# Packed attention, mish layer and top-1 experts on one core: float32 gate logits on four column tiles, a planner that charges two engines for overlap, and a last half that ends by output quarter

## The chip, the cores and the metric

One core of a Trainium2 chip. TensorE (PE; PEld is its weight load) multiplies, VectorE (DVE), ScalarE (ACT) and GpSimd (POOL) work element by element, SyncE (SP) issues the DMAs. The metric is device time in microseconds (us), as the median of several runs. One further execution was profiled; all rows below are of it.

## The reference

```python
def _attn_ref(q, k, v, p):            # 8 batches, 8 heads, 576 tokens, head size 64, 32 packed queries
    p_packed = sm_attn(p, k, v)       # softmax attention
    return sm_attn(q, p_packed, p_packed)
...
def _moe_ref(x, w_in, w_out):         # 4608 tokens, 512 -> 2048 -> 512
    h = x @ w_in
    sp = np.where(h > 20.0, h, np.log1p(np.exp(np.minimum(h, 20.0))))
    return (h * np.tanh(sp)) @ w_out
...
def _moe2_ref(x, w_gate, w1, w2):     # 8 experts, 512 -> 1024 -> 512
    logits = x @ w_gate
    expert_idx = np.argmax(logits, axis=1)
    probs = softmax(logits); gate_w = probs[np.arange(N), expert_idx]
    for e in range(E):
        mask = expert_idx == e
        out[mask] = gate_w[mask, None] * (np.maximum(x[mask] @ w1[e], 0.0) @ w2[e])
```

All is float32. The inputs q, k and p are eight times the drawn ones.

## The kernel before

Tokens are worked in 16 halves of 288 (a half of a batch each), features lie on partitions. A float32 product is made from fp32r numbers: an operand is split into a high part (a rounded copy; names ending in h) and a low part (the original minus the high part; names ending in l), and a product takes three matmuls (high by high, high by low, low by high). So every operand costs a copy (`copy_ways`, L234 on ACT, L235 on DVE, L237 on POOL) and a subtraction (`tensor_ways`, L246, on DVE or POOL).

- The start (to about 130 us) loads the first layer's weights, which come as 64-bit words, splits them (`sgn` L402, `wi` and `a` L407/L410, `woh`, `wol`) and folds the packed values into them (`w_ps` L447, `wp` L450).
- Stage B (to about 783 us) runs the first layer for all halves: `h` (L562), mish on ACT and DVE (`z` L607, then `g` split into two parts), and the output product `x2p` (L575). Its result `x2f` goes to DRAM. Around half 6 the gates of halves 0 and 1 are worked.
- Stage C runs the second layer. For each batch one expert, the one that most of its tokens choose, is loaded (`eraw`) in eight pieces and split into `exh` and `exl`. A step is one eighth of the hidden features for one half: `h_p` (12 matmuls, L835), `g` high on ACT (L842), `g` low on DVE (`moe2_lo`, L847), then `y` (12 matmuls in four output quarters d, L855). After eight steps `os` (L861) scales the four quarters by the gate weight, and a DMA (issued at L255) writes them. The tokens of other experts are worked by a loop at the program's end, behind a branch (L1007).
- A gate: `gate_mm` (L684) multiplies x2 by the gate weights, `gate_copy` (L690) moves the logits to SBUF, `gate_turn` (L696) turns them so that tokens lie on partitions, and small DVE operations (from L702) find the maximum and the softmax weight.

The order on every engine comes from a planner (`Plan`): each step has engines that may do it, with a cost in ns for each, a due time, and buffers of rings that it takes and frees. The planner simulates the engines, and the program is written out in the order that results. A changed cost therefore moves work of every engine.

Of the kernel before, what the change touches and what calls it, by code (L numbers as in the profile page):

```python
# [45 lines left out]
class Plan:  # L46
# [26 lines left out]
    def run(self):  # L73
# [24 lines left out]
        for _ in range(len(self.steps)):  # L98
# [60 lines left out]
def packed_attention_moe_kernel(ctx, tc, pT, kT, v_main, v_tail, qT, w_in, w_out, wg, w1, w2, out):  # L159
# [48 lines left out]
    tot_i = const.tile([1, 1], I32, name="tot_i")  # L208
    wg_f = const.tile([128, 4, 8], F32, name="wg_f")
    wg16 = const.tile([128, 4, 66], F32R, name="wg16")  # L210

# [468 lines left out]
    def gate_mm(i):  # L680
        l_p, n = tile_of("o", [66, TK], name="l_p"), 0
        for d in range(4):
            for x in range(2):
                T.matmul(out=l_p, lhsT=wg16[:, d], rhs=x2s[i][x][:, d], start=(n == 0), stop=(n == 7))  # L684
                n += 1
        gst[i] = l_p

    def gate_copy(i):
        l_s = tile_of("ls", [16, TK])
        S.activation(out=l_s, in_=gst[i][0:16], func=AF.Copy)  # L690
        gst[i] = l_s

    def gate_turn(i):
        t_p = tile_of("o", [96, 3, 16], name="lt_p")
        for t in range(3):
            T.transpose(t_p[:, t, :], gst[i][:, 96 * t:96 * t + 96], ident[0:16, 0:16])  # L696
        gst[i] = t_p

    def gate_max(i):
        sg = rings["sg"]  # L700
        lg = sg.tile([96, 3, 8], F32, tag="lg", name="lg")
        V.tensor_reduce(out=lg, in_=gst[i].rearrange("p t (a e) -> p t e a", a=2), axis=AX.X, op=ALU.add)  # L702
# [65 lines left out]

    def gate(i, x2, free_x2, due, exp_after=(), exp_before=None):
# [4 lines left out]
        tu = step("PE", 93, lambda: gate_turn(i), after=[cp], takes=[("o", ("t", i))], frees=[("ls", i)], due=due)  # L774
        mx = step("DVE", 600, lambda: gate_max(i), after=[tu], frees=[("o", ("t", i))], due=due)
# [35 lines left out]
    def get_expert(b, gate_of, due_of, after=()):  # L811
        fe = step("SP", 100, lambda: find_e(b), after=[found[b], gate_of(0), *after], due=due_of(0) - 8 * US)
        for k, (p, part) in enumerate(pieces):
            due = due_of(k)
            key = ("x", b, p, part)
            ld = step("SP", 0, lambda p=p, part=part: ex_load(b, ev[b], p, part), after=[fe, gate_of(k)],
                      takes=[("raw", key)], nbytes=524288, due=due - 6 * US)
            ring = ("wa", "wb")[p // 2]
            hi = plan.step(copy_ways(lambda p=p, part=part: ex_hi(b, p, part), lambda p=p, part=part: er[b, p, part], 1024),
                           after=[ld] + ex_done.get((b, p), [])[:1],  # L820
                           takes=[(ring, ("e", b, p, x)) for x in "hl"] * (part == 0), due=due)
            lo = plan.step(tensor_ways(lambda p=p, part=part: ex_t[b, p][1][:, 2 * part:2 * part + 2], lambda p=p, part=part: er[b, p, part],
                                       lambda p=p, part=part: r32(ex_t[b, p][0][:, 2 * part:2 * part + 2]), ALU.subtract, 1024),
                           after=[hi], frees=[("raw", key)], due=due)
            ex_done[b, p] = ex_done.get((b, p), []) + [hi, lo]
# [36 lines left out]

    gms, y_in, y_out = {}, {}, {}

# [4 lines left out]
    def moe2(n, due):  # L869
# [11 lines left out]
        lo = step("DVE", 369, lambda: moe2_lo(i, f), after=[hi], frees=[("h", ("y", n))], due=due)  # L881
        for d in range(4):
            y_out[n, d] = step("PE", 399, lambda d=d: moe2_out(b, i, f, d),
                               after=ex_done[b, 2 + c] + [lo, y_out.get((n - 1, d))],
                               takes=[("acc", ("y", i, d))] * (f == 0),
                               frees=[g] + [("wb", ("e", b, 2 + c, x)) for x in "hl"]
                               * (hf == 1 and o == 3), due=due + 2 * TC + TC // 3, lag=500)
        if early:
# [26 lines left out]
    for m, (which, c) in enumerate(ORDER):  # L915
# [13 lines left out]
    wg_zero = step("Pool", 600, lambda: G.memset(wg16.rearrange("p k e -> p (k e)").bitcast(F32), 0.0), due=20 * US)  # L929
    wg_load = dma(16384, lambda: wg_f, lambda: wg, due=60 * US)  # L930
    wg_done = step("DVE", 100, lambda: V.tensor_copy(out=wg16[:, :, 0:8], in_=wg_f), after=[wg_load, wg_zero], due=60 * US)
    wg_done = step("DVE", 100, lambda: V.tensor_tensor(out=wg16[:, :, 8:16], in0=wg_f, in1=r32(wg16[:, :, 0:8]),
                                                       op=ALU.subtract), after=[wg_done], due=60 * US)

    attend(0, None, at(-10))
    for i in range(NH):
# [11 lines left out]
        if i == 6:  # L948
            for m in range(2):
                key = "g", m  # L950
                ld = dma(589824, lambda m=m: x2_load(m), lambda m=m: x2_d[halves[m]], after=[after_in(n0), x2_st[m]],
                         takes=[("x2f", key)], due=at(n0 + 8 * m))
                sp = split_x2(m, key, "raw", [ld], at(n0 + 8 * m + 4))
                b_steps.extend([ld, *sp, *gate(m, key, x2_at("raw", key), at(n0 + 8 * m + 8), sins[2 * i + 1], trig_after[2 * i + 2])])

# [26 lines left out]
    for i in range(NH):  # L982
# [6 lines left out]
        if b > 0:  # L989
            gate(i, ("x2", i), [], C0 + (8 * i - 14) * TC)  # L990
            if hf == 1:
# [93 lines left out]
```

## Time and profile before

| what | value |
| --- | --- |
| median of 3 runs | 1234.04 us (1233.6 to 1234.16) |
| profiled execution, its own time | 1231.74 us |
| its span, first to last instruction | 1229.9 us |
| mean granted TensorE clock | 0.982 of full speed |
| PE busy | 1181.8 us, 96% of the span |
| DVE, ACT, POOL busy | 56%, 50%, 25% of the span |

A row of the timeline gives the start in us, the time that the row covers, engine, line, operation, output and inputs by the program's names, tile shape, and how many instructions it joins; in brackets the idle time before it and what ended it. Matmuls overlap: a 288-column matmul lasts 0.29 us, while the next one starts 0.13 us after it.

### The profile page before, as it was taken

The page shows a single profiled execution, that of the slowest core. Times are in us where ns is not written, and L with a number is a line of the kernel's source. Part 1 is how long each engine was busy: PE and PEld are TensorE (multiplying, and loading weights), DVE is VectorE, ACT ScalarE, POOL GpSimd, SP SyncE. Part 2 cuts the span into 40 slices and gives each one's busy share as a digit, 9 for nine tenths or more (in the row PEclk, how much of TensorE's full clock was granted, in tenths as well). Part 3 has the DMA queues.
Part 4 walks back from the last instruction along what each step waited for, and adds up shares of the span by engine and source line. Part 5 has one row for each costly group of instructions (what it writes and reads, how often), then busy time and mean ns, then how long its engine had stood idle before and what let it go on. Part 6 is the DMA issues. An engine that isn't in the chain of part 4 may idle for free.

```text
span 1229.9 us, 23514 instructions
## 1 busy us (share of the span) xinstructions
PE 1181.8 (96%) x9632; PEld 1094.6 (89%) x9633; DVE 688.1 (56%) x1231; ACT 611.3 (50%) x1263; POOL 307.8 (25%) x285
## 2 busy tenths in 40 slices
PE   5788999999999999999999998999999999999997
PEld 1557899899899898998998998999999999999997
DVE  5988745645555555455445546356556574746442
ACT  3638777776786786776877866211111111111110
POOL 2555211112131121121121224023324050404210
PEclk9878999999999999999999999999999999999999
DMA  8755420420521320322222031143414141523401
GB/s 305 273 202 203 185 108 1 185 108 1 223 90 52 152 108 30 156 108 76 110 108 108 1 142 54 51 137 144 162 64 186 59 185 42 204 72 134 156 31 42
DMA packets 35098, 146.23 MB, mean 119 GB/s; under 512 B 4264, under 2 KB 4392, under 8 KB 30888
## 3 DMA queue, kind: packets, MB, share of 16 engines
q1 hardware_dynamic: 34984, 144.66, 31.9%
q8 instruction: 78, 1.28, 0.4%
q14 instruction: 36, 0.29, 0.1%
HBM read 121.52 MB, written 23.12 MB: 118 GB/s over the span
## 4 chain that ended last, share of the span: by engine, by line
PE 76%; DVE 11%; DMA 4%; issue 4%; POOL 2%; SPq 1%; ACT 1%; DVEq 0%; ACTq 0%; POOLq 0%
PE x2p L575 32%; PE h L562 16%; PE y L855 11%; PE h_p L835 10%; DVE exl L246 3%; DMA eraw<-w 3%; PE w_ps L447 3%; POOL sgn L402 1%; PE o L311 1%; DVE g L847 1%; PE o L278 1%; PE o L494 1%; PE l_p L684 1%; DVE z L607 1%; POOL exh L237 1%
## 5 line engine op out<-in xcount | busy, mean ns | idle before, releaser
L575 PE MATMUL x2p<-g,woh 128*128 128x288 f32 x2048 | 424.4, 300 | 10.6 <-DVE g L246 5.6
L575 PEld LDWEIGHTS x2p<-g,woh 128*128 128x128 f32 x2048 | 331.8, 190 | 35.6 <-issue 18.8
L575 PE MATMUL x2p<-g,wol 128*128 128x288 f32 x1024 | 305.0, 298 | 2.4 <-DVE wol L246 2.4
L562 PE MATMUL h<-hl,wp 128*128 128x288 f32 x1536 | 240.6, 304 | 6.9 <-DVE wp L450 2.8
L562 PEld LDWEIGHTS h<-hl,wp 128*128 128x128 f32 x1536 | 217.7, 194 | 30.4 <-ACT hs L234 13.9
L237 POOL TENSOR_SCALAR g<-z 128x576 fp32r<-128x576 f32 x123 | 106.9, 877 | 462.4 <-DVE z L607 287.0
L842 ACT ACTIVATE g<-h_p 128x288 fp32r<-128x288 f32 x128 | 52.5, 411 | 325.6 <-PE h_p L835 304.4
L855 PE MATMUL y<-g,exh 128*128 128x288 f32 x1024 | 211.1, 298 | 3.0 <-DVE os L861 2.9
L575 PEld LDWEIGHTS x2p<-g,wol 128*128 128x128 f32 x1024 | 194.8, 190 | 2.9 <-DVE wol L246 2.9
L855 PEld LDWEIGHTS y<-g,exh 128*128 128x128 f32 x1024 | 162.6, 188 | 7.0 <-issue 4.7
L579 ACT ACTIVATE z<-h 128x288 f32<-128x288 f32 x256 | 105.5, 412 | 119.6 <-PE h L562 112.8
L607 DVE TENSOR_TENSOR z<-z,hs 128x576 f32<-128x576 f32 x128 | 96.7, 787 | 101.0 <-ACT z L604 101.0
L835 PE MATMUL h_p<-x2h,exh 128*128 128x288 f32 x512 | 152.3, 297 | 0.7 <-DVE g L847 0.7
L835 PE MATMUL h_p<-x2l,exh 128*128 128x288 f32 x512 | 151.1, 295 | 0.0
L835 PE MATMUL h_p<-x2h,exl 128*128 128x288 f32 x512 | 150.7, 294 | 0.0
L855 PE MATMUL y<-g,exl 128*128 128x288 f32 x512 | 150.4, 294 | 0.0
L847 DVE SCALAR_TENSOR_TENSOR g<-h_p,g 128x288 fp32r<-128x288 f32 x128 | 57.9, 452 | 154.7 <-ACT g L842 154.7
L237 POOL TENSOR_SCALAR exh<-eraw 128x1024 fp32r<-128x1024 f32 x63 | 101.6, 1631 | 140.3 <-DMA eraw<-w 111.4
L246 DVE TENSOR_TENSOR g<-z,g 128x576 fp32r<-128x576 f32 x128 | 106.8, 849 | 30.4 <-POOL g L237 30.2
L246 DVE TENSOR_TENSOR exl<-eraw,exh 128x1024 fp32r<-128x1024 f32 x62 | 100.7, 1653 | 29.1 <-issue 14.5
L234 ACT ACTIVATE hs<-h 128x288 f32<-128x288 f32 x256 | 104.7, 409 | 0.0
L835 PEld LDWEIGHTS h_p<-x2h,exh 128*128 128x128 f32 x512 | 96.0, 187 | 1.7 <-DVE g L847 1.3
(132 smaller groups left out, 1368.5 us busy)
## 6 DMA issues: line engine op xcount, KB each, us to landing
eraw<-w SPq DMA_DIRECT2D x64, 512.0 KB, 6.3
wi<-wi_d SPq DMA_DIRECT2D x28, 1024.0 KB, 6.3
x2f<-x_d SPq DMA_DIRECT2D x18, 576.0 KB, 4.0
raw<-kT SPq DMA_DIRECT2D x16, 576.0 KB, 8.3
q<-qT SPq DMA_DIRECT2D x16, 576.0 KB, 5.7
x_d<-x2f SPq DMA_DIRECT2D x16, 576.0 KB, 3.2
out<-os SPq DMA_DIRECT2D x16, 576.0 KB, 3.0
raw<-v_main SPq DMA_DIRECT2D x16, 512.0 KB, 8.3
```

What stands on the lines that cost most here:

```text
L234: ways = [("ACT", (51 if psum else 93) + 0.833 * n, on(lambda d, x: S.activation(out=d, in_=x, func=AF.Copy))), ("DVE", 69 + (1.03 if psum ...
L237: ways.append(("Pool", 160 + 0.835 * n, on(lambda d, x: G.tensor_scalar(out=d, in0=x, scalar1=1.0, scalar2=1.0, op0=ALU.mult, op1=ALU.mult))))
L246: engine.tensor_tensor(out=d, in0=a(), in1=b(), op=op)
L447: T.matmul(out=t[i][quarter(x)], lhsT=pk[own[i], b, x], rhs=w_i[c][own[i], x], start=True, stop=True)
L562: T.matmul(out=h, lhsT=wp_t[b, c][:, xw, kt, 128 * o:128 * o + 128], rhs=a2[i][:, xa, kt], start=(m == 0), stop=(m == 5))
L575: T.matmul(out=accs[i, d], lhsT=w_o[c][xw][:, o, 128 * d:128 * d + 128], rhs=tiles[n]["g"][:, xg, k], start=(f == 0 and m == 0), stop=(f = ...
L579: S.activation(out=part(n, "z", k), in_=tiles[n]["p", k], func=AF.Tanh, scale=0.5)
L607: g0 = step("DVE", 669, lambda n=n, z=z: V.tensor_tensor(out=z(), in0=z(), in1=tiles[n]["hs"], op=ALU.mult), after=[si, *hc[n]], frees=[(" ...
L835: T.matmul(out=h_p, lhsT=ex_t[ek, c][xw][:, k, 128 * o:128 * o + 128], rhs=x2s[xk][xx][:, k], start=(n == 0), stop=(n == 11))
L842: S.activation(out=h[:, 0], in_=hc[xk, f], func=AF.Relu)
L847: V.scalar_tensor_tensor(out=h[:, 1], in0=h_p, scalar=0.0, in1=r32(h[:, 0]), op0=ALU.max, op1=ALU.subtract)
L855: T.matmul(out=accs[xk, d], lhsT=ex_t[ek, 2 + c][xw][:, o, 128 * d:128 * d + 128], rhs=hc[xk, f][:, xh], start=(f == 0 and n == 0), stop=( ...
```

## The change

The gate's logits are no longer made from the fp32r parts of x2. Four float32 matmuls, one for each quarter d of the 512 features, multiply `x2f` itself by 32 weight columns (8 of the gate, 24 of zeros), and each writes its own 32 partitions of `l_p`. The copy to SBUF takes 128 partitions in place of 16. `gate_turn` multiplies by a small matrix `pick`, which sums the four groups of partitions while it turns. The gates of halves 0 and 1 need no split of x2. The low parts of the first expert have DVE as their only engine. In the last half the outputs of the last two steps are written by d, with a DMA for each d. The planner adds 30% of the overlap to a DVE step that overlaps POOL work and 50% to a POOL step, and some step costs and due times differ.

```diff
+    SLOWED = dict(DVE=0.3, Pool=0.5)
...
+                if e in self.SLOWED:
+
+                    other = "Pool" if e == "DVE" else "DVE"
+                    both = min(cost, max(0.0, free_at[other] - now))
+                    cost += self.SLOWED[e] * both
+                    free_at[other] += self.SLOWED[other] * both
...
-    wg_f = const.tile([128, 4, 8], F32, name="wg_f")
-    wg16 = const.tile([128, 4, 66], F32R, name="wg16")
+    wg_f = const.tile([128, 4, 32], F32, name="wg_f")
+    nc.vector.memset(wg_f, 0.0)
+    pick = const.tile([128, 8], F32, name="pick")
+    nc.vector.tensor_reduce(out=pick, in_=ident.rearrange("p (d e) -> p e d", d=4)[:, 0:8], axis=AX.X, op=ALU.add)
...
-        l_p, n = tile_of("o", [66, TK], name="l_p"), 0
+        l_p = tile_of("o", [128, TK], name="l_p")
         for d in range(4):
-            for x in range(2):
-                T.matmul(out=l_p, lhsT=wg16[:, d], rhs=x2s[i][x][:, d], start=(n == 0), stop=(n == 7))
-                n += 1
+            T.matmul(out=l_p[quarter(d)], lhsT=wg_f[:, d], rhs=x2f[i][:, d], start=True, stop=True)
...
-        t_p = tile_of("o", [96, 3, 16], name="lt_p")
+
+        t_p = tile_of("o", [96, 3, 8], name="lt_p")
         for t in range(3):
-            T.transpose(t_p[:, t, :], gst[i][:, 96 * t:96 * t + 96], ident[0:16, 0:16])
+            T.matmul(out=t_p[:, t], lhsT=gst[i][:, 96 * t:96 * t + 96], rhs=pick, start=True, stop=True)
...
-        mm = step("PE", 981, lambda: gate_mm(i), after=x2_split_done[x2] + [wg_done], takes=[("o", ("l", i))],
-                  frees=free_x2, due=due)
+        mm = step("PE", 850, lambda: gate_mm(i), after=[ld, wg_done], takes=[("o", ("l", i))], frees=[("x2f", key)], due=due,
+                  share=0.8)
...
-                                       lambda p=p, part=part: r32(ex_t[b, p][0][:, 2 * part:2 * part + 2]), ALU.subtract, 1024),
+                                       lambda p=p, part=part: r32(ex_t[b, p][0][:, 2 * part:2 * part + 2]), ALU.subtract, 1024, b > 0),
...
-        for d in range(4):
-            y_out[n, d] = step("PE", 399, lambda d=d: moe2_out(b, i, f, d),
-                               after=ex_done[b, 2 + c] + [lo, y_out.get((n - 1, d))],
+        last, ahead[n] = i == NH - 1 and f > 5, (lo, g)
+        for d, m in [(d, m) for d in range(4) for m in ((n - 1, n) if last else (n,))] * (not last or f == 7):
+            lo, g = ahead[m]
+            y_out[m, d] = step("PE", 399, lambda d=d, f=m % 8: moe2_out(b, i, f, d),
+                               after=ex_done[b, 2 + c] + [lo, y_out.get((m - 1, d))] + [ahead[n][0]] * last,
...
-        dma(589824, lambda: out[b, hf], lambda: accs[i], after=en, frees=[("os", i)], due=due)
+        if not last:
+            dma(589824, lambda: out[b, hf], lambda: accs[i], after=en, frees=[("os", i)], due=due)
+            return
+        for d in range(4):
+            dma(147456, lambda d=d: out[b, hf][:, d], lambda d=d: accs[i][:, d], after=[en[d]], frees=[("os", i)], due=due)
```

First place, PE at the first gate, in stage B. Before, the eight matmuls of `l_p` alternate between the high and the low part of x2 (the first two of them are shown):

```order
L562 MATMUL h<-hl,wp 128x288 x24
L684 MATMUL l_p<-x2h,wg_164 66x288
L684 MATMUL l_p<-x2l,wg_164 66x288
...
L575 MATMUL x2p_4161<-g,woh 128x288 x2
L575 MATMUL x2p_4161<-g,wol 128x288
L696 MATMUL lt_p<-ident,ls 96x16 x3
```

The same place in the changed kernel:

```order
L571 MATMUL h<-hl,wp 128x288 x6
L692 MATMUL l_p<-x2f,wg_f 32x288 x4
L571 MATMUL h<-hl,wp 128x288 x12
L704 MATMUL lt_p<-pick,ls 96x8 x3
L584 MATMUL x2p_4060<-g,woh 128x288 x2
```

Four matmuls of 32 weight columns stand for eight of 66, and the turn has 8 columns in place of 16 and contracts over 128 partitions in place of 16.

Second place, the end of stage B, DVE and POOL. Before, DVE first and then POOL (`exl` and `exh` are the first expert's parts, `g` and `z` belong to the last steps of the first layer):

```order
L246 TENSOR_TENSOR exl<-eraw,exh 128x1024 x3
L607 TENSOR_TENSOR z<-z,hs 128x576 x2
L235 CAST g<-z 128x576 x2
L246 TENSOR_TENSOR g<-z,g 128x576 x2
...
L237 TENSOR_SCALAR exh<-eraw 128x1024 x4
L246 TENSOR_TENSOR exl<-eraw,exh 128x1024
L237 TENSOR_SCALAR exh<-eraw 128x1024
L246 TENSOR_TENSOR exl<-eraw,exh 128x1024
```

The changed kernel, DVE and then POOL at the same place:

```order
L255 TENSOR_TENSOR exl<-eraw,exh 128x1024 x3
L616 TENSOR_TENSOR z<-z,hs 128x576 x2
L244 CAST g<-z 128x576
L255 TENSOR_TENSOR g<-z,g 128x576 x2
...
L246 TENSOR_SCALAR exh<-eraw 128x1024 x4
L246 TENSOR_SCALAR g<-z 128x576
L246 TENSOR_SCALAR exh<-eraw 128x1024
L246 TENSOR_SCALAR g<-z 128x576
```

POOL's two `exl` are gone, and one of DVE's two copies to `g` has gone to POOL. On PE, the first step of the second layer (12 matmuls of `h_p`) stood behind the last `x2p`; it now stands ahead of the last 32 groups of `x2p`:

```order
L584 MATMUL x2p_8861<-g,woh 128x288 x2
L584 MATMUL x2p_8861<-g,wol 128x288
L843 MATMUL h_p<-x2h,exh 128x288
L843 MATMUL h_p<-x2l,exh 128x288
L843 MATMUL h_p<-x2h,exl 128x288
...
L584 MATMUL x2p_8829<-g,woh 128x288 x2
L584 MATMUL x2p_8829<-g,wol 128x288
```

Third place, DVE in stage C, over the four steps ahead of an expert's first `os`. Before:

```order
L847 SCALAR_TENSOR_TENSOR g_10315<-h_p,g_10315 128x288
L246 TENSOR_TENSOR exl<-eraw,exh 128x1024 x2
L847 SCALAR_TENSOR_TENSOR g_10356<-h_p,g_10356 128x288
L246 TENSOR_TENSOR exl<-eraw,exh 128x1024 x2
L847 SCALAR_TENSOR_TENSOR g_10396<-h_p,g_10396 128x288
L246 TENSOR_TENSOR exl<-eraw,exh 128x1024 x2
L847 SCALAR_TENSOR_TENSOR g_10431<-h_p,g_10431 128x288
L246 TENSOR_TENSOR exl<-eraw,exh 128x1024 x2
L861 TENSOR_TENSOR os<-y_10172,gm 128x288
```

The changed kernel at the same place:

```order
L855 SCALAR_TENSOR_TENSOR g_10278<-h_p,g_10278 128x288
L255 TENSOR_TENSOR exl<-eraw,exh 128x1024 x3
L855 SCALAR_TENSOR_TENSOR g_10318<-h_p,g_10318 128x288
L244 CAST exh<-eraw 128x1024
L855 SCALAR_TENSOR_TENSOR g_10356<-h_p,g_10356 128x288
L255 TENSOR_TENSOR exl<-eraw,exh 128x1024 x2
L855 SCALAR_TENSOR_TENSOR g_10392<-h_p,g_10392 128x288
L255 TENSOR_TENSOR exl<-eraw,exh 128x1024 x2
L869 TENSOR_TENSOR os<-y_10127,gm 128x288
```

Of an expert's eight `exl` seven stay on DVE, three of them in a row, and DVE makes one `exh`; the eighth `exl` goes to POOL, which makes four `exh` in place of eight, and ACT makes the other three.

## Rows read from the trace of the kernel before

**Rows 1.** Windows: us, busy us (instructions) of each engine, PEclk, DMA share, GB/s.

```profile
34.00:100.00 66.00, 50.19 (x290) 35.17 (x288) 59.99 (x83) 36.51 (x72) 39.01 (x41) 0.79 0.70 249
766.00:770.00 4.00, 1.22 (x6) 1.21 (x6) 4.00 (x4) 0.00 (x0) 1.76 (x1) 0.52 0.02 4
```

**Rows 2.** Timeline of PE at the last gate, in stage C.

```profile
1147.94 0.29 PE L684 MATMUL l_p<-x2h,wg 128*66 128x288 f32 x1
...
1149.00 0.43 PE L855 MATMUL y<-g,exh 128*128 128x288 f32 x2
...
1149.67 0.29 PE L855 MATMUL y<-g,exl 128*128 128x288 f32 x1
1149.89 0.31 PE L696 MATMUL lt_p<-ident,ls 16*96 16x16 f32 x3
1150.13 0.53 PE L855 MATMUL y<-g,exh 128*128 128x288 f32 x2
1150.50 0.29 PE L855 MATMUL y<-g,exl 128*128 128x288 f32 x1
```

**Rows 3.** Timeline of PE in stage B, at float32 matmuls of other lines.

```profile
375.54 0.65 PE L311 MATMUL o<-raw,at 128*32 128x64 f32 x32
...
389.13 0.30 PE L575 MATMUL x2p<-g,wol 128*128 128x288 f32 x1
389.35 0.72 PE L494 MATMUL o<-q,pk 64*32 64x288 f32 x16
390.00 0.54 PE L575 MATMUL x2p<-g,woh 128*128 128x288 f32 x2
390.37 0.29 PE L575 MATMUL x2p<-g,wol 128*128 128x288 f32 x1
...
390.90 0.32 PE L737 MATMUL n_p<-oh,ones 96*128 96x48 f32 x2
391.04 0.52 PE L575 MATMUL x2p<-g,woh 128*128 128x288 f32 x2
391.39 0.29 PE L575 MATMUL x2p<-g,wol 128*128 128x288 f32 x1
```

**Rows 4.** Timeline of PE at the end of stage B.

```profile
763.76 0.29 PE L575 MATMUL x2p<-g,wol 128*128 128x288 f32 x1
765.61 0.40 PE L575 MATMUL x2p<-g,woh 128*128 128x288 f32 x1 [1.56 <-DVE g L235]
768.79 0.61 PE L575 MATMUL x2p<-g,woh 128*128 128x288 f32 x1 [2.78 <-DVE g L246]
...
773.00 0.43 PE L575 MATMUL x2p<-g,woh 128*128 128x288 f32 x2
```

**Rows 5.** Timelines of DVE and of POOL at the same place.

```profile
760.71 3.63 DVE L607 TENSOR_TENSOR z<-z,hs 128x576 f32<-128x576 f32 x2
...
769.33 1.41 DVE L607 TENSOR_TENSOR z<-z,hs 128x576 f32<-128x576 f32 x2
...
759.80 3.26 POOL L246 TENSOR_TENSOR exl<-eraw,exh 128x1024 fp32r<-128x1024 f32 x1
```

**Rows 6.** Stage C: waits (us in total, times, longest), and timelines at one boundary between experts.

```profile
PEld y L855 <- issue: 4.7, 7, 1.4
...
1173.26 2.83 DVE L246 TENSOR_TENSOR exl<-eraw,exh 128x1024 fp32r<-128x1024 f32 x2
...
1176.60 0.50 PE L855 MATMUL y<-g,exh 128*128 128x288 f32 x2 [1.20 <-DVE os L861]
```

**Rows 7.** The end: the last DMA's issue, SP's last waits (first and last start), the smallest DMA timed.

```profile
1223.82 0.33 SPq L255 DMA_DIRECT2D out<-os  x1
...
L1007 SPq EVENT_SEMAPHORE  x9: 17/17/17, 1227.9 to 1228.5; - x9
...
pk<-pT SPq DMA_DIRECT2D x1, 64.0 KB, 2.1
```

**Rows 8.** One line's instructions on DVE in the start (duration ns min/median/max).

```profile
L402 DVE TENSOR_SCALAR sgn<-word x2: 858/864/870, 39.1 to 94.8; 128x512 f32<-128x512 f32 x2
```

More of the change, by code (lines that the diff above doesn't have):

```diff
@@ L680, in gate_mm @@
     def gate_mm(i):
-        l_p, n = tile_of("o", [66, TK], name="l_p"), 0
+        l_p = tile_of("o", [128, TK], name="l_p")
         for d in range(4):
-            for x in range(2):
-                T.matmul(out=l_p, lhsT=wg16[:, d], rhs=x2s[i][x][:, d], start=(n == 0), stop=(n == 7))
-                n += 1
+            T.matmul(out=l_p[quarter(d)], lhsT=wg_f[:, d], rhs=x2f[i][:, d], start=True, stop=True)
         gst[i] = l_p
     def gate_copy(i):
-        l_s = tile_of("ls", [16, TK])
-        S.activation(out=l_s, in_=gst[i][0:16], func=AF.Copy)
+        l_s = tile_of("ls", [128, TK])
+        S.activation(out=l_s, in_=gst[i], func=AF.Copy)
         gst[i] = l_s
     def gate_turn(i):
-        t_p = tile_of("o", [96, 3, 16], name="lt_p")
+        t_p = tile_of("o", [96, 3, 8], name="lt_p")
         for t in range(3):
-            T.transpose(t_p[:, t, :], gst[i][:, 96 * t:96 * t + 96], ident[0:16, 0:16])
+            T.matmul(out=t_p[:, t], lhsT=gst[i][:, 96 * t:96 * t + 96], rhs=pick, start=True, stop=True)
         gst[i] = t_p
@@ L701, in gate_max @@
         lg = sg.tile([96, 3, 8], F32, tag="lg", name="lg")
-        V.tensor_reduce(out=lg, in_=gst[i].rearrange("p t (a e) -> p t e a", a=2), axis=AX.X, op=ALU.add)
+        V.tensor_copy(out=lg, in_=gst[i])
         mx = sg.tile([96, 3], F32, tag="mx", name="gmx")
@@ L767, in gate_out, with gate @@
         gst["r", b] = r_s
-    def gate(i, x2, free_x2, due, exp_after=(), exp_before=None):
+    def gate(i, key, ld, due, exp_after=(), exp_before=None):
         b, hf = halves[i]
-        mm = step("PE", 981, lambda: gate_mm(i), after=x2_split_done[x2] + [wg_done], takes=[("o", ("l", i))],
-                  frees=free_x2, due=due)
+        mm = step("PE", 850, lambda: gate_mm(i), after=[ld, wg_done], takes=[("o", ("l", i))], frees=[("x2f", key)], due=due,
+                  share=0.8)
         cp = step("ACT", 291, lambda: gate_copy(i), after=[mm], takes=[("ls", i)], frees=[("o", ("l", i))], due=due)
-        tu = step("PE", 93, lambda: gate_turn(i), after=[cp], takes=[("o", ("t", i))], frees=[("ls", i)], due=due)
+        tu = step("PE", 400, lambda: gate_turn(i), after=[cp], takes=[("o", ("t", i))], frees=[("ls", i)], due=due)
         mx = step("DVE", 600, lambda: gate_max(i), after=[tu], frees=[("o", ("t", i))], due=due)
@@ L861, in moe2_end @@
         V.tensor_tensor(out=accs[xk][:, d], in0=accs[xk, d], in1=gm, op=ALU.mult)
-    gms, y_in, y_out = {}, {}, {}
+    gms, y_in, y_out, ahead = {}, {}, {}, {}
     def g_load(b):
@@ L881, in moe2 @@
         lo = step("DVE", 369, lambda: moe2_lo(i, f), after=[hi], frees=[("h", ("y", n))], due=due)
-        for d in range(4):
-            y_out[n, d] = step("PE", 399, lambda d=d: moe2_out(b, i, f, d),
-                               after=ex_done[b, 2 + c] + [lo, y_out.get((n - 1, d))],
+        last, ahead[n] = i == NH - 1 and f > 5, (lo, g)
[3 more added lines that the diff above has]
+                               after=ex_done[b, 2 + c] + [lo, y_out.get((m - 1, d))] + [ahead[n][0]] * last,
                                takes=[("acc", ("y", i, d))] * (f == 0),
                                frees=[g] + [("wb", ("e", b, 2 + c, x)) for x in "hl"]
-                               * (hf == 1 and o == 3), due=due + 2 * TC + TC // 3, lag=500)
+                               * (hf == 1 and m % 4 == 3), due=due + 2 * TC + TC // 3 + 800 * d * last, lag=500)
         if early:
@@ L928, in packed_attention_moe_kernel @@
                 convert_out(c, o, Q0 + (4 * m + o) * CHUNK)
[L929 to L933, printed above, removed]
+    wg_done = dma(16384, lambda: wg_f[:, :, 0:8], lambda: wg, due=60 * US)
     attend(0, None, at(-10))
@@ L952, in packed_attention_moe_kernel @@
                          takes=[("x2f", key)], due=at(n0 + 8 * m))
-                sp = split_x2(m, key, "raw", [ld], at(n0 + 8 * m + 4))
-                b_steps.extend([ld, *sp, *gate(m, key, x2_at("raw", key), at(n0 + 8 * m + 8), sins[2 * i + 1], trig_after[2 * i + 2])])
+                b_steps.extend([ld, *gate(m, key, ld, at(n0 + 8 * m + 8), sins[2 * i + 1], trig_after[2 * i + 2])])
     late = after_in(N1 - 24)
@@ L989, in packed_attention_moe_kernel @@
         if b > 0:
-            gate(i, ("x2", i), [], C0 + (8 * i - 14) * TC)
+            gate(i, ("x2", i), ld, C0 + (8 * i - 14) * TC)
             if hf == 1:
```

## The prediction

> **What bounds the kernel now.** I read the table of engines and then the windows by stage. PE is busy in 96% of the span, so time can leave in two ways only: PE gets less work, or one of its gaps closes. The gaps lie in four places. In the start DVE works 60.0 of 66 us while PE works 50.2, at 0.79 of the clock [rows 1]: DVE is the bound there. In the middle of stage B PE hardly waits. At the end of stage B it runs dry: after the matmul at 763.76 the next ones start at 765.61 and 768.79 [rows 4]. In stage C the row of waits shows seven gaps ahead of `y`, 4.7 us in all [rows 6]. At the very end only a DMA is under way, from 1223.82 on [rows 7].
>
> **The gates on PE.** There are 16 of them. Now one holds PE from 1147.94 to 1149.00, 1.06 us, for the logits [rows 2]. For the turn I count from 1149.67 to 1150.50: 0.83 us, in which three `y` matmuls start as well; at 0.132 each (1.06 over the gate's eight) they take 0.40, so the turn costs 0.43.
>
> The new form does not occur before for the logits, so I take the nearest rows. `o` of L494 is float32 too, has 32 weight columns and the same 288 columns of data, on eight tiles at once: from 389.13 to 390.37 pass 1.24 us, in which three ordinary matmuls start (0.40), so the group costs 0.84, its entry and exit included [rows 3]. It uses 64 rows of a tile and the gate uses 128; but 32 matmuls of 128*32 tiles with 64 columns cover 0.65 us as well [rows 3], so tiles of full height also run side by side there. I take 0.84: a gain of 0.22. Bounds: 0.65, the time from the group's start at 389.35 to 390.00 [rows 3], if entry and exit overlap other work (gain 0.41); and four matmuls one behind the other (a rival, below).
>
> The Trainium skill's page "TensorEngine Tiling (Array Packing)", Key Properties, speaks against the change: a change of tiling mode drains TensorE, and the change puts 16 more such switches, there and back, into stretches of full-width matmuls. The trace agrees as far as the matmul behind the group starts late, and those prices are inside the 0.84; without any drain the group would cost nearer the 0.65 of its own row.
>
> The turn becomes three float32 matmuls. `n_p` is one of that kind, recorded as two: from 390.90 to 391.39 pass 0.49 us with two ordinary ones in it (0.26), so it costs 0.23 [rows 3]. Three in a row share entry and exit; between 0.43 (no dearer than now) and 0.69 (three apart) I take 0.45, next to the present row, since most of it is entry and exit. Net per gate 0.22 - 0.02 = 0.20, times 16 is **3.2 us**; bounds -0.04 x 16 = -0.6 and 0.41 x 16 = 6.6. The copy on ACT and the `lg` copy on DVE keep their columns; I cost them at nothing, because 1.5 us of `y` and `x2p` work or more stand behind each of them. x2f is held until the gate's matmuls; its next load comes several steps later, so I put no wait there.
>
> **The end of stage B.** DVE worked on a `z` pair for 3.63 us from 760.71 on, while POOL did an `exl` of 3.26 us from 759.80 on; a like pair at 769.33 took 1.41 [rows 5]. So about 2.2 us of DVE time went to overlap with that one, and POOL's second `exl` lies beside the copies to `g` that follow. PE paid three times: 765.61 - 763.76 - 0.13 = 1.72; 768.79 - 765.61 - 0.13 = 3.05; and the clock, which stood at 0.52 in the window behind the gap [rows 1]: 17 matmuls start between 768.79 and 773.00, 4.21 us for what takes 17 x 0.132 = 2.24, so 1.97. Together 6.7. The changed order takes both `exl` off POOL, one of the two copies off DVE, and gives PE 12 matmuls of `h_p` (12 x 0.132 = 1.6 us) ahead of the `x2p` that waited. DVE then needs a `z` pair (1.4), one copy (about 0.8) and one subtraction (about 0.8) behind 760.7: `g` is ready at about 763.7 to 764.3, and PE has work until 763.8 + 1.6 = 765.4. The two extra `exl` on DVE stand behind those. No gap, hence no slow clock: **6.7 us**; bounds 3 (the `h_p` are late, half of the gap stays) and 6.7.
>
> The Trainium skill, page "SBUF — State Buffer", Who interferes with whom, says that DVE and GpSimd share a port pair under an exclusive lock and that the loser blocks for the whole instruction. By that, DVE would have waited 3.26 us for the one POOL operation; what the row shows is 2.2 for the pair. The measured row is used.
>
> **Stage C.** At the boundary shown, DVE still does an `exl` pair (2.83 us from 1173.26) when `os` is wanted, and PE's `y` waits 1.20 for it [rows 6]. Now an expert has eight `exl` on DVE beside eight `exh` on POOL. In the new order it has seven and one `exh`, and POOL and ACT share the rest, so DVE has less to do and less to do it beside. Three `exl` in a row delay a `g` by up to 3 x 1.4 = 4.2 (half of 2.83 each), but now four pairs precede each boundary, and the seven gaps are one for each boundary [rows 6]: PE waits for none of the earlier pairs, because it works two `h_p` ahead, and only what is left over at the `os` costs it time. Of the 4.7 I take **4.0**; bounds -4 (rival below) and 4.7.
>
> **The tail.** From the issue at 1223.82 to SP's semaphore at 1227.9 pass 4.1 us, for 576 KB; the smallest DMA that is timed, 64 KB, landed in 2.1 [rows 7]. The last piece is now 144 KB: between 2.1 and 4.1 I take 2.5, near the small one. **1.6 us**; bounds 0 and 2. The reordered `y` end at the same time, since they are the same matmuls, and the last `os` still stands behind the last `y`.
>
> **The start.** DVE bounds it and its order changes: four `woh` copies and two `sgn` more than before. At 0.87 for a `sgn` [rows 8] and no more for a copy, that is a loss of up to 5.2; DVE's idle time of 6.0 [rows 1] is the most that a better order can win. PE's first matmuls are only regrouped. I take 0, since both bounds have reasons. The other moved work (28 copies to `g` from POOL to DVE in stage B) lies beside a PE that hardly waits, with DVE half idle by the table: 0.
>
> **The sum.** 3.2 + 6.7 + 4.0 + 1.6 = 15.5. The profiled execution took 1231.74 by its own time (1.84 over its span): 1216.2. The median of the runs stands 2.3 above it, and I take that over: **1218.5 us**.
>
> **Rivals.**
> 1. *Column tiles of full height do not run side by side for 288 columns.* Each then takes the group's 0.65 by itself: 4 x 0.65 = 2.6 against 1.06, 16 x 1.54 = 25 us lost, so 1218.5 + 3.2 + 25 = 1247: slower than before. It decides from 4 x 0.51 on, where a gate costs 1 us more and the other gains are spent. The 128*32 row speaks against it, the different column count leaves it open.
> 2. *Stage C gives back what it should win.* The gate stood between the last `h_p` and the first `y` of a half, so a shorter gate lets PE reach the `os` wait sooner; three `exl` in a row, and one on POOL of up to 3.26 that DVE works beside, seven times, make `os` late again. The gaps stay (0 instead of 4.0) and seven gates give back 0.2 each: 1224. By the skill's lock, named above, DVE would block for the whole of each `exl` on POOL, which makes this rival more likely and not dearer; no row of stage C shows such an `exl` yet.
> 3. *The end of stage B only moves its wait:* `h_p` in front waits for the first expert's `exl`, which DVE now makes alone; 3 of 6.7 are won: 1222.
> 4. *The start loses* up to 5.2: 1223.7, or wins up to 6: 1212.5.
> 5. *The new order does not bring what it looks like:* gates 0, stage C 0, 3 at the end of stage B, 1.6 in the tail: 1234.04 - 4.6 = 1229.4.
>
> **How the numbers follow.** Forecast 0.60, rival 1 0.04, rival 2 0.13, rival 3 0.07, rival 4 0.06 for each sign, rival 5 0.04. The forecast's own range by its bounds is 1214 to 1222. With rivals 2, 3 and 4 the range becomes 1210 to 1227, which leaves out rivals 1 and 5 and the far ends of the others, less than 2 in 10. About 0.2% (2.5 us) is what a measurement can tell from no change. Faster by more: all but rival 1, part of rival 5 and combinations of 2 and 4, 0.92; within it 0.04; slower 0.04.
>
> **What the changed profile would show.** Right: `l_p` as one row of eight records covering some 0.7 us, and the turn at 0.4 to 0.5; PE without a gap between 755 and 785 on the old scale, and the clock at 1.00 there; the row "`y` from issue" below 1 us; a last landing about 2.5 us behind its issue. Wrong: `l_p` spread over 2 us (rival 1); `os` still ahead of `y` at the boundaries (rival 2); `h_p` waiting for `exl` near 763 (rival 3); PE's busy time in 34 to 100 lower, or another window at half clock (rival 4).

## The result and the profile after

| | before | changed |
| --- | --- | --- |
| median | 1234.1 us (1233.6 to 1234.6, 4 runs) | 1211.85 us (1211.0 to 1212.5, 4 runs) |
| profiled execution | 1231.74 us | 1212.49 us |
| span | 1229.9 us | 1210.7 us |
| mean granted clock | 0.982 | 0.988 |

The ratio is 0.9819 (95% interval 0.9802 to 0.9836): 22 us faster, where 15.5 were forecast. The time lies inside the range (1210 to 1227), near its low end, and below the 1214 to 1222 that the forecast's own bounds gave.

Where the time went is read by laying the start times of the same PE instructions beside each other. PE runs `h`, `h_p` and `y` in the same numbers in every kernel here, so the 193rd and 1441st matmul of `h`, the 97th and 1441st of `h_p` and the last of `y` cut every trace at the same work. Each number below is the difference of two such starts in a timeline (the first one counts from the span's start, the last one to its end), in us. The 28.5 us from the 1441st `h_p` to the last `y` are the same in all and left out.

| kernel | start | stage B | end of B | stage C | tail |
| --- | --- | --- | --- | --- | --- |
| before | 150.5 | 575.1 | 81.8 | 387.0 | 6.9 |
| changed | 148.1 | 572.7 | 75.7 | 380.4 | 5.3 |
| difference | 2.4 | 2.4 | 6.1 | 6.6 | 1.6 |

The gate: two of the 16 lie in stage B, one in the end of B and 13 in stage C. The timeline of PE of the changed kernel at the last gate, the place that answers to [rows 2]:

```profile
1130.96 0.29 PE L843 MATMUL h_p<-x2h,exl 128*128 128x288 f32 x1
1131.18 0.69 PE L692 MATMUL l_p<-x2f,wg_f 128*32 128x288 f32 x8
1131.81 0.53 PE L863 MATMUL y<-g,exh 128*128 128x288 f32 x2
1132.17 0.29 PE L863 MATMUL y<-g,exl 128*128 128x288 f32 x1
...
1132.56 0.29 PE L863 MATMUL y<-g,exl 128*128 128x288 f32 x1
1132.69 0.59 PE L704 MATMUL lt_p<-pick,ls 128*96 128x8 f32 x6
1133.14 0.51 PE L863 MATMUL y<-g,exh 128*128 128x288 f32 x2
1133.49 0.29 PE L863 MATMUL y<-g,exl 128*128 128x288 f32 x1
```

Read as before: from 1130.96 to 1132.17 pass 1.21 us with three ordinary matmuls in them (0.40), so the logits cost 0.81. From 1132.56 to 1133.49 pass 0.93, less 0.40: the turn costs 0.53. A gate takes 1.34 in place of 1.06 + 0.43 = 1.49, which is 0.15 less, or 2.4 us for 16.

The end of stage B, a window of all engines, then DVE, which answer to [rows 4, 5]:

```profile
755.00:770.00 15.00, 15.00 (x115) 15.00 (x114) 13.30 (x14) 5.73 (x9) 4.43 (x4) 1.00 0.00 1
```

```profile
756.88 1.42 DVE L616 TENSOR_TENSOR z<-z,hs 128x576 f32<-128x576 f32 x2
```

PE is busy in all of the 15 us, at full clock: neither the gap nor the slow clock behind it is there. The `z` pair takes 1.42 in place of 3.63.

Stage C. The boundary between experts that answers to the one in [rows 6], on DVE and PE:

```profile
1156.17 2.35 DVE L255 TENSOR_TENSOR exl<-eraw,exh 128x1024 fp32r<-128x1024 f32 x2
...
1159.03 0.50 PE L863 MATMUL y<-g,exh 128*128 128x288 f32 x2 [0.64 <-DVE os L869]
```

The `exl` pair takes 2.35 (2.83 before), and `y` waits 0.64 for `os` (1.20 before).

The tail, SP's issues of the last half (four) and its last semaphores, which answer to [rows 7]:

```profile
1203.87 3.23 SPq L264 DMA_DIRECT2D out<-os  x4
...
L1016 SPq EVENT_SEMAPHORE  x9: 17/17/17, 1208.4 to 1209.4; - x9
```

The fourth issue starts at 1206.71, and SP's first semaphore comes 1.7 us later (4.1 before). But that issue starts 0.50 after its `os` has ended, because SP is still at the third issue, which takes 1.17 where the first two take 0.33.

### The profile page after: what moved, and what is told of

It is laid out like the page before. It is cut to its first block, busy times and chain, and to the rows that moved or that the text cites. A ratio compares the mean times of both kernels' runs of the same rounds, so it can differ in the third digit from the quotient of the medians.

```text
span 1210.7 us, 23591 instructions
## 1 busy us (share of the span) xinstructions
PE 1169.7 (97%) x9680; PEld 1082.5 (89%) x9681; DVE 682.1 (56%) x1264; ACT 632.0 (52%) x1285; POOL 232.3 (19%) x221
## 3 DMA queue, kind: packets, MB, share of 16 engines
q8 instruction: 78, 1.28, 0.4%
## 4 chain that ended last, share of the span: by engine, by line
PE 81%; DVE 8%; ACT 3%; DMA 2%; issue 2%; POOL 1%; SPq 0%; DVEq 0%; ACTq 0%; POOLq 0%
PE x2p L584 31%; PE h L571 15%; PE y L863 14%; PE h_p L843 14%; PE w_ps L456 3%; DMA eraw<-w 2%; DVE exl L255 1%; DVE z L616 1%; PE o L320 1%; PE o L503 1%; PE l_p L692 1%; DVE exh L244 1%; DVE g L255 1%; POOL sgn L411 1%; PE lt_p L704 1%
## 5 line engine op out<-in xcount | busy, mean ns | idle before, releaser
L246 POOL TENSOR_SCALAR g<-z 128x576 fp32r<-128x576 f32 x94 | 85.2, 906 | 496.7 <-DVE z L616 294.3
L843 PE MATMUL h_p<-x2h,exh 128*128 128x288 f32 x512 | 151.7, 296 | 0.4 <-DVE g L855 0.4
L616 DVE TENSOR_TENSOR z<-z,hs 128x576 f32<-128x576 f32 x128 | 94.2, 768 | 101.5 <-ACT z L613 101.5
L255 DVE TENSOR_TENSOR g<-z,g 128x576 fp32r<-128x576 f32 x128 | 94.5, 757 | 19.0 <-POOL g L246 18.9
L863 PEld LDWEIGHTS y<-g,exl 128*128 128x128 f32 x512 | 96.5, 189 | 0.0
L843 PEld LDWEIGHTS h_p<-x2l,exh 128*128 128x128 f32 x512 | 96.5, 188 | 0.0
```

Of the source, the lines that this page charges most:

```text
L246: ways.append(("Pool", 160 + 0.835 * n, on(lambda d, x: G.tensor_scalar(out=d, in0=x, scalar1=1.0, scalar2=1.0, op0=ALU.mult, op1=ALU.mult))))
L255: engine.tensor_tensor(out=d, in0=a(), in1=b(), op=op)
L616: g0 = step("DVE", 669, lambda n=n, z=z: V.tensor_tensor(out=z(), in0=z(), in1=tiles[n]["hs"], op=ALU.mult), after=[si, *hc[n]], frees=[(" ...
L843: T.matmul(out=h_p, lhsT=ex_t[ek, c][xw][:, k, 128 * o:128 * o + 128], rhs=x2s[xk][xx][:, k], start=(n == 0), stop=(n == 11))
L863: T.matmul(out=accs[xk, d], lhsT=ex_t[ek, 2 + c][xw][:, o, 128 * d:128 * d + 128], rhs=hc[xk, f][:, xh], start=(f == 0 and n == 0), stop=( ...
```

## The experiments

Each part of the change was first made alone on the kernel before, then the changed kernel was varied. Ratios are to the kernel before, on the same chip. Different runs were on different chips, where the kernel before itself took 1232.65 to 1234.1, so medians of two runs are also compared by what each wins against it. The stages of all runs, in us as above:

| kernel | start | stage B | end of B | stage C | tail | median |
| --- | --- | --- | --- | --- | --- | --- |
| b_slowed | 149.6 | 573.0 | 75.9 | 387.4 | 5.6 | 1219.75 |
| b_gate | 151.7 | 574.3 | 81.3 | 390.0 | 6.7 | 1235.76 |
| b_exl | 151.1 | 575.1 | 76.1 | 386.7 | 6.9 | 1226.93 |
| b_tail | 151.2 | 575.3 | 81.3 | 387.9 | 6.5 | 1233.26 |
| a_noslowed | 151.8 | 574.3 | 76.0 | 390.5 | 6.0 | 1229.74 |
| a_nogate | 149.9 | 573.0 | 75.8 | 382.0 | 5.9 | 1218.96 |
| a_hold | 150.1 | 573.0 | 75.9 | 386.9 | 6.1 | 1219.36 |
| a_serial | 150.0 | 575.7 | 77.4 | 402.1 | 4.5 | 1238.61 |
| a_nopool | 151.9 | 574.3 | 75.9 | 380.4 | 4.6 | 1217.53 |
| best_nopool | 148.8 | 572.7 | 75.6 | 376.4 | 4.6 | 1208.78 |
| dose_half | 149.8 | 572.7 | 75.6 | 388.2 | 5.6 | 1222.36 |
| dose2 | 148.6 | 575.7 | 75.4 | 377.2 | 5.5 | 1212.63 |

### The four parts alone

**b_slowed**, the planner's charge alone:

```diff
+    SLOWED = dict(DVE=0.3, Pool=0.5)
...
+                if e in self.SLOWED:
...
+                    cost += self.SLOWED[e] * both
+                    free_at[other] += self.SLOWED[other] * both
```

> The kernel before with the planner's overlap charge alone. Theory A, from the two traces laid beside each other: the charge makes most of the gain, 2.5 us in the start, 2.5 in stage B (the wait of w_ps for the transposed scores, 0.37 once a batch), about 4.6 at the experts' boundaries, and at the end of stage B it puts h_p ahead, for 3 to 6.5: 12 to 16 us faster, near 1220. Rival B: the shorter gate is what relieves stage C, and the two exl taken from POOL what closes the gap at the end of stage B, so that the charge alone gives no more than the start and stage B: 5 us, near 1229.

1219.75, ratio 0.9881 (0.9865 to 0.9898): 14.3 us faster. Stage B (2.1) and the end of B (5.9) are as theory A had them; the start wins 0.9 against the profile of before, or 1.8 against the mean of the six kernels with the old order there. Stage C is not: 387.4, no gain at all in this profile. Much of what it loses is in one place. From the 577th to the 673rd `h_p` PE takes 30.8 us (27.9 before): at 946.78 `y` has waited 1.82 for `os`, and behind that wait the granted clock falls to half, so that 14 matmuls take 3.46 in place of 1.9:

```profile
948.20:951.60 3.40, 3.40 (x17) 3.37 (x16) 2.50 (x12) 0.22 (x1) 0.00 (x0) 0.50 0.76 263
```

The rest of stage C is 2.5 shorter than before, and this execution took 2.1 more than the median of its runs. So theory A holds for stage B and its end, is too high for the start (2.5), and the 4.6 that it gives stage C are not in this profile; what the faster executions win there is in no trace.

**b_gate**, the new gate alone:

```diff
-        l_p, n = tile_of("o", [66, TK], name="l_p"), 0
+        l_p = tile_of("o", [128, TK], name="l_p")
         for d in range(4):
-            for x in range(2):
-                T.matmul(out=l_p, lhsT=wg16[:, d], rhs=x2s[i][x][:, d], start=(n == 0), stop=(n == 7))
-                n += 1
+            T.matmul(out=l_p[quarter(d)], lhsT=wg_f[:, d], rhs=x2f[i][:, d], start=True, stop=True)
...
```

> The kernel before with the float32 gate on column tiles alone; the order of the rest stays nearly as it was. Theory A: 0.245 saved on the logits and 0.10 lost on the turn, 16 times: 2.3 us faster, near 1231.8, less where a shorter gate only reaches the wait for os sooner (down to 0.5). Rival B: the gate no longer waits for the split of x2, and the boundaries in stage C shrink with it: 5 us or more faster.

1235.76, ratio 1.0018 (1.0008 to 1.0028): 1.7 us *slower*. Both theories miss. Stage C takes 3.0 longer although 13 gates save 2. PE's waits for `os` there grow from 2.9 to 4.7 and those for `g` from 0.7 to 2.8. One of the places is seen on DVE and then PE:

```profile
942.20 4.04 DVE L248 TENSOR_TENSOR exl<-eraw,exh 128x1024 fp32r<-128x1024 f32 x2 [0.95 <-POOL exh L239]
946.16 0.45 DVE L848 SCALAR_TENSOR_TENSOR g<-h_p,g 128x288 fp32r<-128x288 f32 x1
...
946.75 0.37 PE L836 MATMUL h_p<-x2h,exh 128*128 128x288 f32 x1 [1.14 <-DVE g L848]
```

A pair of `exl` takes 4.04 beside POOL's `exh`, the low part of `g` comes behind it, and the next `h_p` waits 1.14 for its PSUM buffer. This is the wait of the prediction's second rival, in another order than the one it was written for, and it takes more than the gate's gain.

**b_exl**, the first expert's low parts on DVE:

```diff
-                                       lambda p=p, part=part: r32(ex_t[b, p][0][:, 2 * part:2 * part + 2]), ALU.subtract, 1024),
+                                       lambda p=p, part=part: r32(ex_t[b, p][0][:, 2 * part:2 * part + 2]), ALU.subtract, 1024, b > 0),
```

> The kernel before with the first expert's low parts on DVE alone. h_p stays behind all x2p. Theory A: the overlap of DVE and POOL made the gap at the end of stage B, so it shrinks from 4.8 to about 1 and no slow clock follows: 4 to 6 us faster, near 1229. Rival: DVE has two more exl ahead of the copies and subtractions, the gap stays: no change, or 1 us slower.

1226.93, ratio 0.9945 (0.9929 to 0.9962): 7.1 us faster. The end of stage B shortens by 5.7 (81.8 to 76.1) and no other stage moves by more than 0.6. b_slowed reaches the same 75.9 by another way, with `h_p` put ahead and both `exl` still on POOL. Each of the two edits closes this gap by itself; together they close it once.

**b_tail**, the last half by output quarter:

```diff
+        for d in range(4):
+            dma(147456, lambda d=d: out[b, hf][:, d], lambda d=d: accs[i][:, d], after=[en[d]], frees=[("os", i)], due=due)
...
```

> The kernel before with the last half's outputs by d and four DMAs. Theory A: the last landing is shorter by 1.6 us and nothing else moves: 1232.4. Rival: the small DMAs land no sooner than the large one (their time is latency), or their issues stand in line: 0.5 us at most.

1233.26, ratio 0.9993 (0.9983 to 1.0002): 0.8 us, not clear of zero. Over all profiles the tail took 5.6 to 6.9 in four kernels with one last DMA (before, b_slowed, b_gate, b_exl) and 4.5 to 6.5 in the ten with four, so 1.6 in one pair of profiles was partly luck. The part of the rival on issues that stand in line is seen in the traces: in all ten the third issue takes 0.69 to 2.28 where the first two take 0.33, and the fourth starts behind it, up to 1.63 after its `os`. The three kernels in which the third takes 0.74 or less have the three shortest tails (4.5 to 4.6). Why the third issue is long was not tested.

### The changed kernel with a part undone

**a_noslowed**, all but the charge:

```diff
-    SLOWED = dict(DVE=0.3, Pool=0.5)
...
-                    cost += self.SLOWED[e] * both
-                    free_at[other] += self.SLOWED[other] * both
```

> The changed kernel without the planner's overlap charge. If the parts add up as they were measured alone (gate +1.7, exl -7.1, tail -0.8): 1228. If the gate needs the charge to pay, because exl pairs keep standing ahead of the g that PE waits for: the same 1228, with PE's waits for g and os in stage C as large as in the kernel with the gate alone. If the gate pays by itself once POOL is relieved: 1223.

1229.74, ratio 0.9965 (0.9952 to 0.9977), against 1228 for the sum of the parts (6.2 won by the parts, 3.5 here, each against the kernel before on its own chip). Stage C stays bad (390.5), as with the gate alone. Its waits of PE, with the total, the times and the longest:

```profile
PE y L856 <- DVE os L862: 4.8, 7, 1.4
...
PE h_p L836 <- DVE g L848: 2.5, 3, 1.1
```

In the changed kernel the waits for `os` and `g` are 1.1 and 0.4. So in stage C the gate does not pay in this order; a_nopool, below, shows what it needs.

**a_nogate** and **a_hold**, the changed kernel with the old gate; in a_hold x2f is also held until the gate has run:

```diff
-            gate(i, ("x2", i), [], C0 + (8 * i - 14) * TC)
+            gate(i, ("x2", i), [("x2f", ("x2", i))], C0 + (8 * i - 14) * TC)
```

> The changed kernel with the old gate: eight fp32r matmuls, x2f free after the split. Theory C: the new gate's worth lies mostly in the order, since x2f is held until the gate and the next half's split can then no longer stand at the boundary between halves: without it stage C loses 4 to 7 us, 1217 to 1219. Rival D: only the gate's own 2.3 us is lost: 1214.

> The same old gate, but x2f is freed by the gate's matmuls in place of the split, as with the new gate. Theory C: the split of the next half moves behind the gate on DVE as in the changed kernel, stage C is as fast as there, and only the arithmetic differs, 16 x 0.144 = 2.3 us: 1214. Rival D: no difference from the kernel with the old gate that frees x2f early.

1218.96 (1216.9 to 1223.5; ratio 0.9889, 0.9861 to 0.9917) and 1219.36 (1217.0 to 1222.3; ratio 0.9874, 0.9851 to 0.9896): no difference. Theory C falls: holding the buffer brings nothing, although DVE's order at the boundaries then is nearly that of the changed kernel. In its profile a_hold loses 5.6 us within one expert (31.3 and 28.6 for its two halves, 27.3 and 27.0 for those of the expert before): PE waits 1.28 for the numbers of the chosen expert and 2.33 for a late `g`, and behind these waits its granted clock is 0.51 for 3.5 us. The times of this kernel and of a_nogate also spread over 5.3 and 6.6 us, those of the changed kernel over 1.5. In the profile of a_nogate stage C takes 382.0, only 1.6 more than in the changed kernel, which is the gate's own price (13 x 0.15 = 2.0). But that execution is the fastest of its four, and the medians differ by 7 (by 8, set against the kernel before on each chip). The slower executions of a_nogate were not traced; that they lose as a_hold does, by a wait and the clock behind it, is likely and not shown.

**a_serial**, the gate's four matmuls on one column tile:

```diff
-        l_p = tile_of("o", [128, TK], name="l_p")
+        l_p = tile_of("o", [32, TK], name="l_p")
         for d in range(4):
-            T.matmul(out=l_p[quarter(d)], lhsT=wg_f[:, d], rhs=x2f[i][:, d], start=True, stop=True)
+            T.matmul(out=l_p, lhsT=wg_f[:, d], rhs=x2f[i][:, d], start=(d == 0), stop=(d == 3))
...
```

> The changed kernel with the gate's four float32 matmuls one behind the other on one column tile (they add up in PSUM there, and the turn contracts 32 partitions). This is the price of the first rival of the prediction. If a 128x32 float32 matmul with 288 columns takes what a round of four takes side by side (0.53), a gate's logits cost 4 x 0.53 + 0.3 = 2.4 in place of 0.82: 16 x 1.6 = 25 us slower, 1237. If the rounds are half that: 8 us slower, 1220.

1238.61, ratio 1.0032 (1.0017 to 1.0048): 26.8 us over the changed kernel (27.6, set against the kernel before on each chip). A gate's eight records of `l_p`, at 1157.73, cover 2.13 us in place of 0.69. Stage C grows by 21.7, which is 1.67 for each of 13 gates; 1.44 of it is that row. So the four tiles do run side by side in the changed kernel, and the first rival was priced nearly right: by its sum it lies 28 over the forecast.

### Is it the overlap of DVE and POOL?

**a_nopool**, no charge, but for the later experts no `exh` on POOL (their `exl` had none there without the charge):

```diff
-            hi = plan.step(copy_ways(lambda p=p, part=part: ex_hi(b, p, part), lambda p=p, part=part: er[b, p, part], 1024),
+            hi = plan.step(copy_ways(lambda p=p, part=part: ex_hi(b, p, part), lambda p=p, part=part: er[b, p, part], 1024)[:3 - (b > 0)],
```

> The changed kernel without the overlap charge, but the later experts' exh and exl never go to POOL: ACT makes the exh, DVE all exl. The overlap theory: with the gate held x2f and an uncharged order, stage C took 390.5 us because DVE's exl took 1.8 to 2.0 each beside POOL's exh; without POOL they take 1.1 to 1.2 and stage C needs about 381, so 1229.7 - 9 = 1220.5. Rival: three exl in a row ahead of a g that PE waits for, or the later split, are to blame, and the time stays at 1228 to 1230.

1217.53, ratio 0.9874 (0.9858 to 0.9890): 12.2 us under a_noslowed, by one line (11.6, set against the kernel before on each chip: 15.1 won and 3.5). Stage C goes from 390.5 to 380.4, as in the changed kernel. The `exl` on DVE, first in a_noslowed, then in a_nopool, with ns min/median/max:

```profile
L248 DVE TENSOR_TENSOR exl<-eraw,exh x64: 1211/1692/2067, 736.3 to 1173.0; 128x1024 fp32r<-128x1024 f32 x64
```

```profile
L248 DVE TENSOR_TENSOR exl<-eraw,exh x64: 1212/1226/2057, 736.4 to 1161.8; 128x1024 fp32r<-128x1024 f32 x64
```

The median falls from 1692 to 1226 ns and the waits for `os` are gone. The other thing that the line changes, where an `exl` gets its `exh` from, does not explain it: DVE waits longer for ACT's `exh` (25.9 us, 26 times, between 800 and 1200) than it did for POOL's (15.0, 18 times). The overlap theory holds for stage C.

**dose_half** and **dose2**, half and twice the charge:

```diff
-    SLOWED = dict(DVE=0.3, Pool=0.5)
+    SLOWED = dict(DVE=0.15, Pool=0.25)
```

```diff
-    SLOWED = dict(DVE=0.3, Pool=0.5)
+    SLOWED = dict(DVE=0.6, Pool=1.0)
```

> The changed kernel with half the charge (0.15 and 0.25). The order puts h_p ahead as with the full charge and moves copies to g from POOL to DVE, but leaves 63 exh on POOL, as without any charge. Theory: the end of stage B is as with the full charge, stage B at 572 to 573, and stage C as bad as without it, about 390: near 1222. Rival: POOL's exh are not the cause in stage C, and it comes out near 382: 1213.

> The changed kernel with twice the charge (0.6 and 1.0). The order keeps 33 exh and 16 exl on POOL and puts 24 matmuls of h_p ahead of the last x2p. Stage C as in the changed kernel, the start a matter of another order: 1210 to 1215. Rival: too high a charge overloads ACT, whose copies to g come late: slower than 1216.

Half: 1222.36, ratio 0.9913 (0.9896 to 0.9929). Its order leaves the experts' `exh` on POOL, and as expected stage C is bad (388.2) while start, stage B and end of B are within what the kernels with the full charge show. The `exl` median is 1687 ns again. Twice: 1212.63, ratio 0.9839 (0.9822 to 0.9855), near the changed kernel (20.0 won on its chip, where that won 22.2 on another); stage C is 3 us better (377.2), stage B 3 us worse (575.7).

**best_nopool**, the changed kernel with no `exh` and no `exl` of the later experts on POOL:

```diff
-            hi = plan.step(copy_ways(lambda p=p, part=part: ex_hi(b, p, part), lambda p=p, part=part: er[b, p, part], 1024),
+            hi = plan.step(copy_ways(lambda p=p, part=part: ex_hi(b, p, part), lambda p=p, part=part: er[b, p, part], 1024)[:3 - (b > 0)],
...
-                                       lambda p=p, part=part: r32(ex_t[b, p][0][:, 2 * part:2 * part + 2]), ALU.subtract, 1024, b > 0),
+                                       lambda p=p, part=part: r32(ex_t[b, p][0][:, 2 * part:2 * part + 2]), ALU.subtract, 1024, False),
```

> The changed kernel, charge included, and again no exh or exl of the later experts on POOL. If overlap is what is left at the boundaries (y waits 1.1 for os, and DVE waits for POOL's exh), 1 us faster than the changed kernel: 1211. If DVE's eight exl in place of seven, or ACT's copies ahead of g, cost more than that: 1212 to 1215.

1208.78 (1208.5 to 1209.4), ratio 0.9807 (0.9791 to 0.9823): 3.1 us under the changed kernel, where 1 was expected. Set against the kernel before on each chip it is 1.6 (23.9 won and 22.2), and the two intervals overlap, so the medians do not show that it is faster. The traces do show a better stage C: it takes 376.4 (380.4 in the changed kernel), and PE waits for no `os` and no `g` there. ACT carries the 57 `exh` at 1.06 us each without PE noticing.

## Why the prediction was right, point by point

- **The gates, 3.2 forecast, 2.4 measured.** The logits were sized right (0.84 forecast, 0.81 measured), and L494 was the right row for them. The turn was not: 0.53 in place of 0.45. Five of its six records start 0.085 us before the next matmul, so the turn is more than one entry and exit.
- **The end of stage B, 6.7 forecast, 6.1 measured.** The mechanism and the clock were right. What it did not see is that two edits do the same: either is enough (b_exl, b_slowed).
- **Stage C, 4.0 forecast, about 4.6 measured** (6.6 less 2.0 for 13 gates). The cause named, overlap of DVE with POOL's `exh`, is shown by a_nopool and dose_half. The upper bound of 4.7, read from one row of waits, was too low: in its trace best_nopool wins another 4.0 in this stage. Nor does a row of waits hold what the clock costs behind them: in b_slowed and a_hold waits of about 2 us cost some 1.5 more at half clock. The sign that I named, the row "`y` from issue" below 1 us, was a bad one. It stays at 4.5, in seven gaps of at most 0.8 (1.4 before), while the time is won; PE's own waits for `os` (2.9 before, 1.1 after) tell more than its loader's.
- **The tail, 1.6 forecast, 1.6 in the profiles, 0.8 in the medians of the part alone.** The last piece did land sooner, 1.7 us from its issue to SP's semaphore where 2.5 was forecast. What the sum put at nothing is the line of issues: the fourth starts 0.50 late in the changed kernel, behind a third issue of 1.17, and 1.20 late in b_tail.
- **The step that failed is "The start: 0" and, with it, the moved work in stage B: 0.** Each stage is 2.4 us shorter. In the start the five other kernels with the old order there (b_gate, b_exl, b_tail, a_noslowed, a_nopool) need 151.1 to 151.9, and the eight with a charge 148.1 to 150.1, so 2.0 us, the difference of the two means, are the charge's; a_serial, whose start has the changed kernel's order, needs 150.0, so the rest is the spread of single executions. Which wait went there was not tested. In stage B "PE hardly waits" passed over a wait that comes back in most batches. The timeline of PE there, before and after:

```profile
214.60 1.45 PE L447 MATMUL w_ps<-wi,pk 64*32 64x512 f32 x16
215.98 0.40 PE L575 MATMUL x2p<-g,woh 128*128 128x288 f32 x1
```

```profile
212.11 1.09 PE L456 MATMUL w_ps<-wi,pk 64*32 64x512 f32 x16
213.13 0.40 PE L584 MATMUL x2p<-g,woh 128*128 128x288 f32 x1
```

  `w_ps` splits into two parts because its second PSUM buffer is still being read by a transposition on DVE; 1.38 us to the next `x2p` become 1.02. That is so in five places of stage B (1.8 us), and a sixth wins 0.33; with the 0.3 of the two gates there, that is the 2.4. b_slowed, with the old gate, has the first two gains and wins 2.1. PE's busy share hides such a wait, since the records of a waiting group overlap.
- **The carry-over of 2.3 us between profile and median failed.** The profiled execution of before lay 2.3 below its median, that of the changed kernel 0.6 above. So 3.0 of the 22.2 us come from there, 19.2 from the stages. No term or bound held this or the 2.4 of stage B: that 1211.85 still lies inside the range, by 1.85, is owed to the width that rival 4 gave it, and is partly luck.
- **Rivals.** The first did not come and was priced nearly right. The wait of the second comes with the gate alone (b_gate) and not in the changed kernel, where the charge takes half of POOL's copies away. Of the fourth, the winning side came in part: 2 of up to 6 us. The third and the fifth did not come.

## What to carry to other kernels

When a planner places work on VectorE and GpSimd as if they were independent, a price for the overlap, or simply keeping one of them out of a stage, can be worth more than saved matmuls: here one line that took `exh` off POOL won 11.6 us (a_nopool against a_noslowed). Test each part of a change alone and with the others: the new gate costs 1.7 us by itself, and two other parts close the same gap. Compare medians from different chips through a kernel that ran on both. Cut the traces at the same work and compare stage by stage; sums of waits mix what costs time with what does not.

## What the runs showed of the hardware

A copy on VectorE that begins while a two-input subtraction runs on GpSimd waits for the end of it. In the changed kernel, DVE and then POOL:

```profile
1149.97 2.53 DVE L244 CAST exh<-eraw 128x1024 fp32r<-128x1024 f32 x1
...
1149.31 2.63 POOL L255 TENSOR_TENSOR exl<-eraw,exh 128x1024 fp32r<-128x1024 f32 x1 [1.84 <-ACT exh L243]
```

POOL's subtraction ends at 1151.94 and the copy at 1152.50, 0.56 us later; without POOL (a_nopool, L237) the same copy takes 0.69 from start to end. All seven such copies of the changed kernel end 0.55 after POOL's `exl` (before rounding), whether they began 0.15 or 0.66 into it. So the copy waited for POOL's instruction to its end. This is the rule of the Trainium skill's page "SBUF — State Buffer", Who interferes with whom: the shared port pair is a lock, and the loser blocks. The prediction set the rule aside because a `z` pair lost 2.2 us beside a POOL operation of 3.26 [rows 5]. That was the rule misread: POOL's `exl` ended at 763.06, 2.35 after the pair began, and 2.35 plus the 1.41 of an undisturbed pair is 3.76, close to the 3.63 measured; the first `z` by itself took 2.96. The trace agrees with the rule there too.

The slow `exl` of stage C are the same lock changing hands. In the kernel before, DVE and then POOL:

```profile
832.95 2.05 DVE L246 TENSOR_TENSOR exl<-eraw,exh 128x1024 fp32r<-128x1024 f32 x1 [0.58 <-POOL exh L237]
...
832.87 1.05 POOL L237 TENSOR_SCALAR exh<-eraw 128x1024 fp32r<-128x1024 f32 x1
```

The `exh` ends at 833.92 and the `exl` at 835.00, 1.08 later by these rows and 1.07 before rounding. From 800 us on, all 39 `exl` of that kernel that begin while an `exh` runs end 1.07 after it, and all 41 `exh` that begin while an `exl` runs end 0.90 to 0.92 after that. So when both engines have a row of these, they take turns: 1.98 us for one of each, where alone they take 1.22 and 1.05. Working side by side saves 0.3 us of 2.27. The planner charges 30% and 50% of an overlap; what these traces show is one instruction waiting for the other.

A gap of TensorE can cost twice. In b_slowed a wait of 1.82 is followed by a stretch at the lower of the clock's two levels (0.50 of full speed from 948.20 to 951.60, and 1.00 from there to 955.00), in which PE works without a gap and loses 1.6 more. a_hold shows the same behind a wait of 2.33. In the kernel before, whose waits for `os` are 1.2 at most, stage C has no such stretch.
